# Windowed attention gated with a routed feed-forward layer: a searched table of key shifts for the list scheduler, values projected per chunk, loads in pieces, a hinted branch

## The chip, the cores and the metric

The kernel runs on one core of a Trainium2 chip. The metric is the device time of one execution in microseconds (us), median of the runs shown. The engines are named as the profile names them: PE (TensorE matrix multiplies) and PEld (its weight loads), DVE (VectorE), ACT (ScalarE), POOL (GpSimd), and SP, which here issues nearly all DMA transfers. PE takes its instructions in program order, and so do the others; an instruction that waits holds back all behind it on its engine.

## The reference

`x` is 2048 x 512 in bf16. Two branches of it are mixed by a gate per row.

```python
def _A_ref(x, wqkv, wo):                      # H = 32 heads, Dh = 16, window W = 256
    q, k, v = split_heads(x @ wqkv)
    scores = einsum(q, k) * Dh ** -0.5
    mask = (i - j >= 0) & (i - j < 256)
    p = softmax(where(mask, scores, -1e9))
    return merge_heads(p @ v) @ wo
def _B_ref(x, w_r, w_gate, w_up, w_down):     # F = 1792, C = 8
    r = x @ w_r
    idx = argsort(-r)[:8]                     # 8 rows of 2048
    y = (silu(x[idx] @ w_gate) * (x[idx] @ w_up)) @ w_down
    return x with y * sigmoid(r[idx]) added to rows idx
g = sigmoid((x * gate_w).sum(-1))
out = g * _A_ref(x) + (1 - g) * _B_ref(x)
```

## The kernel before

The 32 heads are worked in four chunks `c` of 8 heads (128 features). A chunk has 64 units; unit `u = 64c + kb` takes 32 keys (block `kb`), the 288 queries that can see them, and the 8 heads as two halves of four. For a unit, PE makes two matmuls into two PSUM banks (`s_unit`, L612: the keys stand in a block-diagonal tile `Kbd`, so that 4 heads x 32 keys fill 128 rows), ACT takes the exponential of both banks in one instruction into the tile `PT` (L619), and POOL multiplies the edges of the window by a mask for two units at a time (L626). Scores have two bank pairs in turn, so the scores of unit u wait until the exponential of unit u-2 has read its banks. `PT` is a ring of 40 slots, two for a unit: the exponential of unit u writes where unit u-20 stood, and must wait until `pv` (L647, probabilities times values for a tile `j` of 128 queries) has read that. A unit of key block kb is read last by tile j = kb/4 + 2.

Around this run the other items, each into one of two PSUM bank pairs (banks 4-5 and 6-7), which is free again when DVE has copied its result out: `xt` (transpose of x, L468), `qk_pair` (queries and keys of a chunk for 512 rows, L528; DVE then writes `QT` and `Kbd`, L506, L509, L514), `v_pair` (values, L571), `pv` (then a reciprocal L662 and a product L666 on DVE), `tr` (transpose of the attention output, L682, L687), `wo_pair` and `wo_one` (output projection, L702 and L718, then DVE's `out_evict` L693 and a DMA to the output, L695), and the routed branch: `z_item` (L739), `top_item` (8 largest, L762 to L776), `gu_item` (L799), `down_item` (L827). For `v_pair`, x is the stationary side: the values of two chunks (256 features) for 512 rows are made at once, copied to `Vn` (L583), written to a scratch `vsc` in DRAM (L586) and read back into the layout that `pv` wants, `Vbd` (L594, `v_read`). `pair` issues a projection as two phases of 64-row halves on the two halves of the array, one pair of matmuls per schedulable step.

The order of the work on each engine comes from a list scheduler (`Sched.schedule`). Every step has an engine, an assumed cost and a key; of the steps that are ready on an engine the one with the least key goes next, and on PE a score that is about to be ready is not delayed by a step that would end more than `TOL` = 100 ns late. The keys are written in units of `u` (`qk_pair` has d - 24, where d is the unit that needs it, and so on). Waits on semaphores follow from the order.

SP's queue before: x, the weights, `wo`, a copy of the whole of x to `xc` in DRAM (L413), then the value writes and reads, and three loads of 1792 KB for the routed branch (L818), each one DMA.

The end: DVE checks that all reciprocals lie in a range (L911 to L913), a matmul sums the check (L915), DVE writes `flag` (L916), SP waits for all transfers and engines, all engines meet, load `flag` and branch: a general program follows in the code that is jumped over when the flag says that all was in range.

## Time and profile before

| | us |
|---|---|
| median of 3 runs (217.71, 216.78, 219.93) | 217.71 |
| the profiled execution | 218.59 |
| its span, first to last instruction | 216.4 |
| mean granted TensorE clock | 0.885 |
| busy in the span: PE / ACT / DVE / POOL | 174.0 / 146.6 / 118.7 / 89.6 |
| the 256 exponentials (L619), busy | 140.3 |

The profiled execution is 0.88 us above the median, and 2.2 us longer than its span, since the time has something around the instructions. PE's busy time is that of pipelined instructions with modelled ends, so 80% busy does not say that PE has only 20% to spare or that it is the bound; what bounds is read from who waits for whom at each place.

### The profile page before, as it was taken

The page shows a single profiled execution, that of the slowest core. Times are in us where ns is not written, and L with a number is a line of the kernel's source. Part 1 is how long each engine was busy: PE and PEld are TensorE (multiplying, and loading weights), DVE is VectorE, ACT ScalarE, POOL GpSimd, SP SyncE. Part 2 cuts the span into 40 slices and gives each one's busy share as a digit, 9 for nine tenths or more (in the row PEclk, how much of TensorE's full clock was granted, in tenths as well). Part 3 has the DMA queues.
Part 4 walks back from the last instruction along what each step waited for, and adds up shares of the span by engine and source line. Part 5 has one row for each costly group of instructions (what it writes and reads, how often), then busy time and mean ns, then how long its engine had stood idle before and what let it go on. Part 6 is the DMA issues. An engine that isn't in the chain of part 4 may idle for free.

```text
span 216.4 us, 10097 instructions
## 1 busy us (share of the span) xinstructions
PE 174.0 (80%) x4598; PEld 111.0 (51%) x4599; DVE 118.7 (55%) x301; ACT 146.6 (68%) x266; POOL 89.6 (41%) x142
## 2 busy tenths in 40 slices
PE   2999548699687779986999868999899799998850
PEld 1655236465555535653667544645666455556410
DVE  5659507515617691827066183725663567575880
ACT  6677503686557797975779846656899899977000
POOL 3043401344134497653345432427365555645000
PEclk9999955969857976999599997999999799999995
DMA  6999436902410000045021472110330023254131
GB/s 172 334 267 423 129 77 126 302 24 56 103 32 4 5 3 5 3 129 216 3 55 32 138 232 57 38 44 5 83 108 3 3 100 100 80 169 151 52 123 32
DMA packets 27663, 21.72 MB, mean 100 GB/s; under 512 B 14896, under 2 KB 26432, under 8 KB 27584
## 3 DMA queue, kind: packets, MB, share of 16 engines
q1 hardware_dynamic: 26496, 20.75, 33.2%
q8 instruction: 37, 0.61, 1.1%
q10 hardware_dynamic: 1056, 0.26, 0.5%
q14 instruction: 10, 0.08, 0.1%
q0 software_dynamic: 64, 0.02, 0.0%
HBM read 16.13 MB, written 6.43 MB: 104 GB/s over the span
## 4 chain that ended last, share of the span: by engine, by line
PE 51%; ACT 19%; DVE 11%; DMA 9%; issue 6%; SPq 1%; DVEq 0%
ACT f_PT L619 19%; PE f_ps L612 12%; PE f_ps L647 11%; PE f_ps L528 10%; PE f_ps L571 6%; DMA f_vsc<-f_Vn 5%; PE f_ps L702 4%; DVE f_Kbd L514 3%; DVE f_Vn L583 3%; PE f_ps L468 2%; DMA f_xw<-in_A_x_dram 2%; PE f_ps L827 2%; PE f_ps L549 2%; DVE f_outt L693 1%; DVE f_Kr L509 1%
## 5 line engine op out<-in xcount | busy, mean ns | idle before, releaser
L619 ACT ACTIVATE f_PT<-f_ps 128x576 bf16<-128x576 f32 (+7 forms) x256 | 140.3, 625 | 49.8 <-PE f_ps L647 29.9
L626 POOL TENSOR_TENSOR f_PT<-f_PT,f_MK 128x256 bf16<-128x256 bf16 (+1 forms) x128 | 85.4, 669 | 109.3 <-ACT f_PT L619 108.4
L612 PE MATMUL f_ps<-f_QT,f_Kbd 64*128 64x288 bf16 (+7 forms) x512 | 77.9, 299 | 11.5 <-ACT f_PT L619 7.1
L647 PE MATMUL f_ps<-f_Vbd,f_PT 64*128 64x34 bf16 x2880 | 56.1, 179 | 13.2 <-DMA f_Vbd<-f_vsc 5.6
L647 PEld LDWEIGHTS f_ps<-f_Vbd,f_PT 64*128 64x128 bf16 x2880 | 51.8, 96 | 25.4 <-issue 14.7
L612 PEld LDWEIGHTS f_ps<-f_QT,f_Kbd 64*128 64x128 bf16 x512 | 25.9, 96 | 40.3 <-ACT f_PT L619 30.8
L528 PE MATMUL f_ps<-f_XT,f_W 64*128 64x512 bf16 x240 | 41.6, 413 | 0.5 <-issue 0.3
L509 DVE CAST f_Kr<-f_ps 128x512 bf16<-128x512 f32 x15 | 10.4, 691 | 27.1 <-PE f_ps L528 27.0
L571 PE MATMUL f_ps<-f_W,f_XT 64*128 64x256 bf16 x256 | 23.5, 299 | 0.2
L514 DVE TENSOR_SCALAR f_Kbd<-f_Kr,f_hm 128x512 bf16<-128x512 bf16 (+1 forms) x64 | 22.7, 417 | 0.0
L583 DVE CAST f_Vn<-f_ps 128x256 bf16<-128x256 f32 x32 | 11.4, 419 | 16.8 <-PE f_ps L571 16.7
L662 DVE RECIPROCAL f_RC<-f_ps 128x16 f32<-128x16 f32 x32 | 8.0, 248 | 18.9 <-PE f_ps L647 18.9
L571 PEld LDWEIGHTS f_ps<-f_W,f_XT 64*128 64x128 bf16 x256 | 13.5, 104 | 4.3 <-PE f_ps L571 1.2
L528 PEld LDWEIGHTS f_ps<-f_XT,f_W 64*128 64x128 bf16 x240 | 12.2, 100 | 6.5 <-issue 2.5
L693 DVE SCALAR_TENSOR_TENSOR f_outt<-f_ps,f_g_f,f_XT 128x512 bf16<-128x512 f32 x16 | 11.4, 746 | 5.6 <-PE f_ps L702 5.6
L702 PE MATMUL f_ps<-f_wo,f_OT 64*128 64x512 bf16 x96 | 13.8, 377 | 0.7 <-DVE f_outt L693 0.7
L666 DVE TENSOR_TENSOR f_On<-f_ps,f_RC 128x256 bf16<-128x256 f32 x32 | 13.5, 422 | 0.8
L468 PE MATMUL f_ps<-f_ident,f_xw 128*128 128x128 bf16 x64 | 6.2, 265 | 5.0 <-DMA f_xw<-in_A_x_dram 4.2
L506 DVE CAST f_QT<-f_ps 128x512 bf16<-128x512 f32 x15 | 10.2, 680 | 0.0
L687 DVE COPY f_OT<-f_ps 128x512 bf16<-128x512 bf16 x16 | 6.6, 412 | 3.6 <-PE f_ps L682 3.5
L468 PEld LDWEIGHTS f_ps<-f_ident,f_xw 128*128 128x128 bf16 x64 | 5.0, 120 | 6.5 <-issue 4.8
L920 ACT COPY f_sg<-f_ones_f 1x1 f32<-1x1 f32 x1 | 0.2, 191 | 10.8 <-DVE flag L916 10.8
(88 smaller groups left out, 86.9 us busy)
## 6 DMA issues: line engine op xcount, KB each, us to landing
f_vsc<-f_Vn SPq DMA_DIRECT2D x8, 272.0 KB, 3.5
f_XT<-f_xc SPq DMA_DIRECT2D x4, 512.0 KB, 4.4
out_dram<-f_outt SPq DMA_DIRECT2D x16, 128.0 KB, 1.7
f_xw<-in_B_w_gate_dram SPq DMA_DIRECT2D x1, 1792.0 KB, 10.1
f_xw<-in_B_w_up_dram SPq DMA_DIRECT2D x1, 1792.0 KB, 8.3
f_xw<-in_B_w_down_dram SPq DMA_DIRECT2D x1, 1792.0 KB, 8.1
f_xw<-in_A_x_dram SPq DMA_DIRECT2D x3, 512.0 KB, 6.7
f_Vbd<-f_vsc SPq DMA_DIRECT2D x32, 34.0 KB, 1.8
```

Of the source, the lines that this page charges most:

```text
L468: ins = e.transpose(pb[:, o:o + 128], x_sb[:, a1 + ai, kc * 128:kc * 128 + 128], ident[:])
L514: dve(lambda e, h=h, k0=k0, q=q: e.tensor_scalar(out=Kbd[:, c % 2, k0:k0 + w8, h, :], in0=Kr[:, tc % 2, 32 * w8 * q:32 * w8 * q + 32 * w8] ...
L528: return e.matmul(bank((A, B)[which]), W[R, kc, f0:f0 + 128], XT[R, kc, ts], start=st, stop=False, skip_group_check=True, tile_position=(R ...
L571: return e.matmul(bank((A, B)[b])[:, 256 * i:256 * i + 256], XT[R, kc, 128 * a:128 * a + 128], W[R, kc, f0:f0 + 256], start=st, stop=False ...
L583: dve(lambda e, dst=dst, b=b, cc=cc: e.tensor_copy(out=dst, in_=bank((A, B)[b]).rearrange("p (i c s h d) -> p c h s i d", i=2, c=2, s=2, h ...
L612: ins = e.matmul(bank(b0 + s)[:, 0:n], Kbd[R, c % 2, kb, :, :].rearrange("p h k -> p (h k)"), QT[R, c % 2, 32 * kb:32 * kb + n], start=Tru ...
L619: act(lambda e: e.activation(out=dst, in_=ps[:, b0:b0 + 2, 0:n], func=ACT.Exp, scale=0.25), r=[T(b0), T(b0 + 1)], w=[("P", slot // 2)], n= ...
L626: pool(lambda e: e.tensor_tensor(out=v, in0=v, in1=m, op=ALU.mult), r=[("P", sl // 2), ("P", sl // 2 + 1)] + MKR, w=[("Pm", sl // 4)], cos ...
L647: ins = e.matmul(bank((A, B)[rg])[:, col:col + 34], PT[R, o0:o0 + 128], Vbd[R, c % 2, :, kb % 4, kb // 16, s, (kb // 4) % 4, :], start=(kb ...
L666: dve(lambda e: e.tensor_tensor(out=dst, in0=both(h_)[:, :, 0:68 * nj].rearrange("p b (j g d) -> p b j g d", d=17, g=4)[:, :, :, :, 0:16], ...
L693: dve(lambda e: e.scalar_tensor_tensor(out=outt[:, a % 4, :], in0=bank(b), scalar=g_f[:, a:a + 1], in1=xb[:, a, :], op0=ALU.mult, op1=ALU. ...
L702: return e.matmul(bank((A, B)[o]), OT[R, c, 128 * a:128 * a + 128], wo[R, c, :], start=st, stop=False, skip_group_check=True, tile_positio ...
```

## The change

1. `SHIFT`, a table of 289 numbers, is added to the keys before scheduling: one for each item, key and engine. The scores and what has a key under -800 are left out. Two of its lines stand in the diff.
2. `qk_pair` and `wo_pair` make their matmuls 256 columns wide instead of 512 (`NQ = 2`), twice as many. `v_pair` makes the values of one chunk for 1024 rows, 128 columns wide, instead of two chunks for 512 rows; `Vn`, `vsc` and `v_read` follow (16 writes of half the size, 32 reads). `Kr` has four buffers instead of two.
3. Loads: the weights of later chunks, `wo`, the copy to `xc` and the three loads of the routed branch are cut in pieces, and each piece waits for the exponential of a unit (`gate(u)`).
4. The tail: the last four tiles of `pv`, `tr` and `wo_one` are cut finer (tiles 14 and 15 apart, the first three of the four matmuls of `wo_one` as steps of their own with an earlier key), and the check of the reciprocals is made per chunk (`rc_check`).
5. The end: the branch is a conditional jump over the general program, with a hint on PE that is placed 40 steps before PE's last; SP's waits for all transfers stand behind the branch.
6. `_track`: a wait is now also made for a write after a write or a read on the same engine (not on PE).

```diff
+        for op in self.log:
+            if op.key >= -800 and op.tag != "s":
+                op.key += SHIFT.get(_group(op), 0.0)
...
-                if op.eng == "pe" or not (raw or op.dma):
+                if op.eng == "pe":
                     continue
...
+                if e == "pe" and i == len(self.ops[e]) - HINT_AT:
+                    self.hint = h.mark_branch_hint_location()
...
-            if e == "sp":
-                for s, tot in enumerate(self.dtot):
-                    if tot > seen["sp"].get(("d", s), 0):
-                        h.wait_ge(self.dsem[s], tot)
...
+HINT_AT = 40
+NQ = 2
+VLEAD = 24
+SHIFT = {
+    "xt/-700/dve": 39.5, "xt/-699.9/pe": 5.5, "xt/-2/pe": 16.5, "xt/-2/dve": -30.5, "xt/-1.9/pe": 3.5, "xt/6/pe": -9.5, "xt/6/dve": -13,
+    "xt/6.1/pe": -13.5, "pair/-16/pe": -9, "v_pair/-16/dve": -108, "v_pair/-15.5/sp": -20, "v_read/-14.4/sp": -43.5, "k_evict/-16/dve": 0.5,
...
-        def v_pair(cp, g, key):
-            f0 = 1024 + 256 * cp
+        def v_pair(c, gg, key):
+            f0 = 1024 + 128 * c
...
-                w=[("P", slot // 2)], n=2 * n, key=u)
+                w=[("P", slot // 2), ("E", u)], n=2 * n, key=u)
...
-            pe(fn, r=WOR + [("OT", c, a) for c in range(4)], w=[T(b)], cost=960, key=key)
+            for c in range(4):
+                pe(lambda e, c=c: e.matmul(bank(b), OT[:, c, 128 * a:128 * a + 128], wo[:, c, :], start=(c == 0), stop=(c == 3)),
+                   r=WOR + [("OT", c, a)], w=[T(b)], cost=217 if c < 3 else 250, key=key if c == 3 else 252)
...
+        at(1.6, lambda: load_w(1, 1, 1, 1, 4000, gate=gate(1)))
+        at(2.6, lambda: load_w(0, 1, 1, 2, 4000, gate=gate(2)))
+        at(10.6, lambda: load_w(2, 1, 1, 10, 4000, gate=gate(10)))
+        for i in range(4):
+            at(46.6 + 4 * i, lambda i=i: load_ff(B_w_gate, i, 46 + 4 * i, gate(46 + 4 * i)))
+            at(62.6 + 2 * i, lambda i=i: copy_x(i, 62 + 2 * i, gate(62 + 2 * i)))
+            at(88.6 + 3 * i, lambda i=i: load_ff(B_w_up, i, 88 + 3 * i, gate(88 + 3 * i)))
+            at(126.6 + 4 * i, lambda i=i: load_down(i, 126 + 4 * i, gate(126 + 4 * i)))
...
+            br = eng.br_cond(bad < 1, "fk_done", "fk_general")
+            if et == mybir.EngineType.PE:
+                br.branch_hint(S.hint)
```

Three places show what moves. The first is SP's queue at the start, behind the loads of x. Before (`f_W` is the projection weights, `f_wo` the output weights, `f_xc` the copy of x, `f_vsc` and `f_Vbd` the value write and read):

```order
L392 DMA f_W<-in_A_wqkv_dram 128x4x384 x2
L392 DMA f_W<-in_A_wqkv_dram 128x4x256
L412 DMA f_wo<-in_A_wo_dram 32x4x512 x4
L451 DMA f_Vbd<-f_Vbd 32x2176 x4
L413 DMA f_xc<-in_A_x_dram 32x32768
L586 DMA f_vsc<-f_Vn 128x8x136
L594 DMA f_Vbd<-f_vsc 32x4x136 x4
```

The same stretch of SP's queue in the changed kernel:

```order
L512 DMA f_Vbd<-f_Vbd 32x2176 x4
L452 DMA f_W<-in_A_wqkv_dram 128x4x128 x2
L644 DMA f_vsc<-f_Vn 128x4x136 x2
L652 DMA f_Vbd<-f_vsc 32x4x272 x4
L452 DMA f_W<-in_A_wqkv_dram 128x4x128
L644 DMA f_vsc<-f_Vn 128x4x136 x2
L652 DMA f_Vbd<-f_vsc 32x4x272 x4
```

Ahead of the first value write stand two weight pieces instead of three large ones, `wo` and the copy of x, which now come later.

The second place is PE around units 44 to 53, in the first chunk. Before, with the scores of unit 44 in the first row and of units 45, 46 and 47 in the L612 rows after it (L528 is the query and key projection of the next chunk, L739 the router's and gate's products, L647 `pv`, L682 `tr`):

```order
L612 MATMUL f_ps<-f_QT,f_Kbd 128x288 x2
L528 MATMUL f_ps<-f_XT,f_W 128x512 x4
L612 MATMUL f_ps<-f_QT,f_Kbd 128x288 x2
L528 MATMUL f_ps<-f_XT,f_W 128x512 x4
L739 MATMUL f_ps<-f_wrg,f_XT 128x2 x128
L647 MATMUL f_ps<-f_Vbd,f_PT 128x34 x96
L612 MATMUL f_ps<-f_QT,f_Kbd 128x288 x2
L682 MATMUL f_ps<-f_ident,f_On 128x64 x8
L612 MATMUL f_ps<-f_QT,f_Kbd 128x288 x2
```

In the changed kernel, units 50 to 53 on PE (the four L670 rows are their scores, L705 `pv`, L795 the router's and gate's products):

```order
L705 MATMUL f_ps<-f_Vbd,f_PT 128x34 x16
L670 MATMUL f_ps<-f_QT,f_Kbd 128x288 x2
L705 MATMUL f_ps<-f_Vbd,f_PT 128x34 x32
L670 MATMUL f_ps<-f_QT,f_Kbd 128x288 x2
L705 MATMUL f_ps<-f_Vbd,f_PT 128x34 x32
L670 MATMUL f_ps<-f_QT,f_Kbd 128x288 x2
L705 MATMUL f_ps<-f_Vbd,f_PT 128x34 x16
L795 MATMUL f_ps<-f_wrg,f_XT 128x2 x16
L670 MATMUL f_ps<-f_QT,f_Kbd 128x288 x2
L795 MATMUL f_ps<-f_wrg,f_XT 128x2 x32
```

The 96 matmuls of one `pv` and the 128 small products stood in one block between the scores of units 45 and 46; they now stand in pieces between the scores of units 49 and 57.

The third place is PE's end, from the scores of the last unit on. Before (L702 is `wo_pair`, L718 `wo_one`):

```order
L612 MATMUL f_ps<-f_QT,f_Kbd 128x32 x2
L702 MATMUL f_ps<-f_wo,f_OT 128x512 x6
L647 MATMUL f_ps<-f_Vbd,f_PT 128x34 x16
L702 MATMUL f_ps<-f_wo,f_OT 128x512 x8
L647 MATMUL f_ps<-f_Vbd,f_PT 128x34 x64
L702 MATMUL f_ps<-f_wo,f_OT 128x512 x8
L682 MATMUL f_ps<-f_ident,f_On 128x64 x8
L702 MATMUL f_ps<-f_wo,f_OT 128x512 x8
L718 MATMUL f_ps<-f_wo,f_OT 128x512 x16
L915 MATMUL f_ps<-f_ones_f,f_okc 1x1
```

In the changed kernel, from the same score on (L761 is `wo_pair`, L775 `wo_one`, L740 `tr`):

```order
L670 MATMUL f_ps<-f_QT,f_Kbd 128x32 x2
L705 MATMUL f_ps<-f_Vbd,f_PT 128x34 x8
L761 MATMUL f_ps<-f_wo,f_OT 128x256 x14
L740 MATMUL f_ps<-f_ident,f_On 128x64 x4
L761 MATMUL f_ps<-f_wo,f_OT 128x256 x2
L241 BRANCH_PREFETCH_HINT
L775 MATMUL f_ps<-f_wo,f_OT 128x512
L761 MATMUL f_ps<-f_wo,f_OT 128x256 x16
L705 MATMUL f_ps<-f_Vbd,f_PT 128x34 x48
L775 MATMUL f_ps<-f_wo,f_OT 128x512 x7
L705 MATMUL f_ps<-f_Vbd,f_PT 128x34 x48
L740 MATMUL f_ps<-f_ident,f_On 128x64 x2
```

Eight more matmuls of `wo_one` follow. Behind the last score stands half as much of `wo_pair` as before (32 matmuls of 256 columns, not 30 of 512), and the sixteen matmuls of `wo_one` are parted by the last two tiles of `pv`.

## The prediction

> **What bounds the kernel now.** I read the page first: the busy times, the chain that ended last, and the group of the exponentials.

> ```profile
> PE 174.0 (80%) x4598; PEld 111.0 (51%) x4599; DVE 118.7 (55%) x301; ACT 146.6 (68%) x266; POOL 89.6 (41%) x142
> PEclk9999955969857976999599997999999799999995
> PE 51%; ACT 19%; DVE 11%; DMA 9%; issue 6%; SPq 1%; DVEq 0%
> L619 ACT ACTIVATE f_PT<-f_ps 128x576 bf16<-128x576 f32 (+7 forms) x256 | 140.3, 625 | 49.8 <-PE f_ps L647 29.9
> ```

> The 256 exponentials keep ACT busy for 140.3 us and cannot be cut by this change, and ACT stands idle for 49.8 us before them. That idle time is what an order can win, with what lies ahead of the first exponential and behind the last. ACT's waits and its timeline tell whose it is.

> ```profile
> ACT f_PT L619 <- PE f_ps L647: 29.9, 11, 11.5
> ACT f_PT L619 <- PE f_ps L612: 18.1, 28, 3.0
> 9.92 4.89 ACT L619 ACTIVATE f_PT<-f_ps 128x576 bf16<-128x576 f32 x8 [0.75 <-PE f_ps L612]
> 17.77 6.63 ACT L619 ACTIVATE f_PT<-f_ps 128x576 bf16<-128x576 f32 x12 [2.96 <-PE f_ps L612]
> 35.93 4.60 ACT L619 ACTIVATE f_PT<-f_ps 128x576 bf16<-128x576 f32 x8 [11.52 <-PE f_ps L647]
> 83.51 1.39 ACT L619 ACTIVATE f_PT<-f_ps 128x576 bf16<-128x576 f32 x2 [0.73 <-PE f_ps L647]
> 129.66 1.19 ACT L619 ACTIVATE f_PT<-f_ps 128x576 bf16<-128x576 f32 x2 [2.90 <-PE f_ps L647]
> 173.29 19.07 ACT L619 ACTIVATE f_PT<-f_ps 128x576 bf16<-128x576 f32 x34 [0.44 <-PE f_ps L612]
> 193.75 3.61 ACT L619 ACTIVATE f_PT<-f_ps 128x576 bf16<-128x576 f32 x7 [1.39 <-PE f_ps L647]
> 197.54 1.76 ACT L619 ACTIVATE f_PT<-f_ps 128x320 bf16<-128x320 f32 x5 [0.18 <-PE f_ps L612]
> ```

> Two kinds of wait. A wait for L647 is the ring: the exponential of unit u may not write before `pv` of tile (kb-20)/4+2 has read the slot. A wait for L612 is a score that came late. Where neither happens, 34 exponentials follow each other in 19.07 us, 0.56 each, with projections and `pv` in between: the last stages show that an order without loss exists. The exponentials run from 9.92 to 199.3 (197.54 and 1.76), 189.4 us; behind them lie 17.1 us. The stages:

> ```profile
> 9.90:70.40 60.50, 47.23 (x1179) 31.75 (x1179) 31.45 (x88) 35.41 (x65) 20.00 (x31) 0.81 0.53 143
> 70.40:114.40 44.00, 36.64 (x1072) 24.00 (x1070) 24.05 (x56) 35.42 (x66) 23.92 (x33) 0.84 0.15 51
> 114.40:161.90 47.50, 42.03 (x1190) 26.23 (x1190) 25.27 (x68) 35.10 (x65) 22.10 (x34) 0.96 0.32 84
> 161.90:199.30 37.40, 34.17 (x998) 20.89 (x998) 23.41 (x55) 34.43 (x64) 20.90 (x33) 0.95 0.28 87
> ```

> Each row is one chunk: its length, then busy PE, PEld, DVE, ACT, POOL, the granted clock, and DMA. ACT works some 35 us in each; the chunks last 60.5, 44.0, 47.5 and 37.4. The granted clock is lowest (0.81, 0.84) where the stalls are.

> **The first value transfer.** The largest stall, 11.52 us at unit 20, is a DMA's.

> ```profile
> 15.41 11.26 DMA f_vsc<-f_Vn
> 28.00 1.84 DMA f_Vbd<-f_vsc
> f_vsc<-f_Vn SPq DMA_DIRECT2D x8, 272.0 KB, 3.5
> 26.69 1.74 SPq L594 DMA_DIRECT2D f_Vbd<-f_vsc  x4
> ```

> The write of the first values took 11.26 us where the eight of them have a median of 3.5, behind 1 MB of weights, `wo` and the 2 MB copy of x. In the changed queue (the first place above) two 128 KB pieces stand there. The new `v_pair` needs twice the rows of x, so I put its copies on DVE half a us later, to 16.0; with 0.5 for the issue, 3.5 for the landing, 1.74 for four reads and 1.84 for the last to land, `pv` has its values at 23.6. The exponential of unit 19 ended at 24.4. So the data is no longer last; what is left at unit 20 is what PE does between, 20 matmuls of `v_pair` and 88 of `pv`, which the rates below make 1.7 us, and 0.3 of latency: 2.0, bounds 1.5 and 4.

> **The blocks on PE.** I went through both orders for one thing: is the `pv` that unit u's ring slot needs placed behind the score of unit u+1? If so, ACT must run empty there. Before there are ten such places, units 20, 44, 60, 124, 148, 152, 156, 164, 172 and 244, and the waits for L647 are eleven, 29.9 us, the eleventh being the 0.73 at 83.51. In the changed order two are left, units 20 and 148: the second place above shows one that went. Unit 148 has 48 matmuls of `pv` behind that score and cost 2.90; I take 2.0, bounds 1 and 3. **Ring: 29.9 becomes 2.0 + 2.0 + 0.7 = 4.7**, bounds 2.5 and 7.7.

> ```profile
> 188.94 0.43 PE f_ps L702 x4
> 148.38 0.44 PE f_ps L571 x8
> 99.18 0.40 PE f_ps L647 x32
> ```

> These give PE's rates where it runs at full clock: 512 columns 107 ns a matmul, 256 columns 55, `pv` 12.5. So `qk_pair` in halves costs the same (480 x 55 against 240 x 107, 26 us each way). A 128-column matmul has no row: by columns it takes 27 ns, and 512 of them 14 us like the 256 before; at worst it takes the 55 of the 256-column row, which adds 14 us to PE. I take the first, since `pv` shows that a weight load can be had every 12.5 ns. What halves buy is that no step between two scores is longer than the 0.43 us that ACT's pitch of 0.56 leaves beside a score.

> [...]

> **Late scores, 18.1 us.** 2.96 is unit 8, which waits for the second projection; that chain keeps its length, and I keep 3.0. The other 15.1 have two sources:

> ```profile
> 35.35 0.39 SPq L818 DMA_DIRECT2D f_xw<-in_B_w_gate_dram  x1
> 40.05 1.88 issue
> 93.76 0.40 SPq L818 DMA_DIRECT2D f_xw<-in_B_w_up_dram  x1
> 100.24 1.98 issue
> PE f_ps L647 <- issue: 5.4, 6, 1.9
> 60.45 0.43 PE L612 MATMUL f_ps<-f_QT,f_Kbd 64*128 64x288 bf16 x2
> 64.77 0.30 PE L612 MATMUL f_ps<-f_QT,f_Kbd 64*128 64x288 bf16 x2
> f_xw<-in_B_w_gate_dram SPq DMA_DIRECT2D x1, 1792.0 KB, 10.1
> ```

> PE stood for 1.88 and 1.98 us with nothing in the profile to wait for, 5 and 6 us behind the issue of a 1792 KB load, of which the first took 10.1 to land. And after a gap PE ran slow for some us: a pair of scores takes 0.43 at 60.45 and 0.30 at 64.77. Fewer gaps make fewer slow stretches, and loads in quarters leave less to stand behind. How much goes cannot be read off; between 3 and 15.1 I take half, 7.5. **Late scores: 3.0 + 7.5 = 10.5.**

> So the exponentials take 140.3 + 4.7 + 10.5 = 155.5, from 9.9 to 165.4, against 199.3.

> **The tail**, from the last exponential to the end:

> ```profile
> 204.60 3.40 PE L718 MATMUL f_ps<-f_wo,f_OT 128*128 128x512 bf16 x15 [0.16 <-issue]
> 208.66 1.40 DVE L693 SCALAR_TENSOR_TENSOR f_outt<-f_ps,f_g_f,f_XT 128x512 bf16<-128x512 f32 x2
> 209.97 0.14 DVE L916 TENSOR_SCALAR flag<-f_ps 1x1 int32<-1x1 f32 x1
> 201.61 8.80 SPq L695 DMA_DIRECT2D out_dram<-f_outt  x8
> out_dram<-f_outt SPq DMA_DIRECT2D x16, 128.0 KB, 1.7
> ```

> Behind the last score the changed PE has 32 matmuls of 256 columns (1.8 us), 16 of `wo_one` (3.4) and 104 of `pv` (1.3) with a few transposes: 6.7 us, against 10.8 before from 199.3 to the last product of DVE at 210.06. The score starts 0.5 ahead of the last exponential; with 0.3 of latency, 0.74 for the last product, and 0.8 for the turns between PE and DVE over tiles 14 and 15, that is 8.0 us behind 165.4. Then the last output: issued until 210.41 before, landed 1.7 later, 2.0 behind DVE. The flag was written at 210.11 and the span ends at 216.4: 6.3 us, of which the landing explains 2.0 and the rest, 4.3, is load and branch. Now the landing is waited for behind the branch, so the two overlap. How much of the 4.3 the hint takes has no row, between 0 and 4.3; if more than 2 go, the landing is last, and I take that: 2.2 with the closing waits. Tail 10.2, against 17.1; bounds 9.2 and 12.5. [...]

> What is added on DVE, 15 short check steps for three of 0.42 to 0.68, and the new same-engine waits lies beside the exponentials; DVE has 24 busy us of 37 in the last chunk to cover it, and if it were not hidden it would cost 2 us at most. Gated pieces stand in SP's queue ahead of value reads that are needed 8 to 30 units (4 to 17 us) later, more than their 3.5 us.

> **The sum.** Span 165.4 + 10.2 = 175.6. The profiled execution lasts 2.2 longer than its span and is 0.9 above the median: 175.6 + 2.2 - 0.9 = **177 us** against 217.7. Its own range: with the low ends (ring 2.5, late scores 5.3, 2 us less busy ACT as fewer exponentials start from rest, tail 9.2) 166; with ring 7.7, late scores 15.0 and a tail of 12.5, 187.

> **Rivals.** (a) *DVE holds the banks.* All items but scores share two bank pairs, freed by DVE. DVE's 118.7 us go into 176, so it would be 67% busy, not 55.

> ```profile
> 168.06 1.60 DVE f_Kbd L514 x4
> PE f_ps L647 <- DVE f_On L666: 0.5, 2, 0.3
> ```

> For it: DVE is 11% of the chain, 24 us, 4 of them in the tail, and at 168.06 the chain runs through the block-diagonal keys. Against it: PE's direct waits for DVE are short. If most of those 20 us come back as late scores, 177 + 17 = 194.
> (b) *Narrow matmuls are not cheaper, and it gets slower.* If a matmul is bound by its weight load and costs what the next wider one does (107 ns at 256 columns, 55 at 128), `qk_pair` gains 26 us, `wo_pair` 10, `v_pair` 14: 50 us on a PE that is busy for 160 between first and last exponential. 210 us of PE work would then set the end: 9.9 + 210 + 10.2 + 1.3 = 231. It decides from some 34 us on, where PE passes what the kernel takes now. Against it stand the 55 ns of the 256-column row.
> (c) *The hint does nothing.* Then load and branch, 4.3, follow the flag, which comes 0.5 to 1 behind the last product: 180.

> **Chances.** My forecast (166 to 187) 0.66; (a), 187 to 205, 0.20; (c), inside that range, 0.06; better than 166, 0.04; (b) 0.04. Eight in ten need about half of (a): 166 to 194. A measurement of this kernel tells some 2% from no change, 213.4 to 222; faster than that are all but (b) and the worst of (a): 0.93, same 0.03, slower 0.04.

> **What would show it.** In the changed profile: the first value write lands in 3 to 5 us and `pv` starts before 25; ACT's waits for L705 fall under 8 us with units 20 and 148 the largest; the four chunks last about 42, 38, 38 and 37 us, and the clock is above 0.9 in the second; the 128-column matmuls come at 27 ns; from the last exponential to the end 10 us, the landing last. The prediction is wrong if ACT still waits over 25 us, for DVE's banks, for late scores at a low clock, or for value reads behind gated loads.

## The result and the profile after

| | before | after |
|---|---|---|
| median, us | 217.95 (216.78 to 219.93, 4 runs) | 203.69 (200.94 to 205.74, 4 runs) |
| the profiled execution / its span | 218.59 / 216.4 | 203.83 / 202.5 |
| exponentials, first start to last end | 9.92 to 199.3 = 189.4 | 9.50 to 187.07 = 177.6 |
| of it ACT waits for `pv` / for late scores | 29.9 / 18.1 | 5.5 / 28.8 |
| last exponential to DVE's last product | 10.8 | 8.15 |
| last product to the end of the execution | 8.5 | 8.6 |

The ratio is 0.9295, 95% interval 0.917 to 0.942: 14 us faster. Forecast were 41 (177.0, range 166 to 194), so the sign held and the size didn't. A second time, with experiments 14 and 15, the changed kernel took 201.37 beside 217.82, ratio 0.9249 (0.9165 to 0.9332). Ratios and intervals here and below leave out runs that lie over 1.5% above the fastest of their kernel, medians don't, so a ratio can differ a little from that of two medians.

The page after: the busy times, the clock, the chain that ended last, the instruction transfers of PE, and from the groups of instructions the one of the exponentials (busy, mean ns, idle before it and for whom).

```profile
PE 166.8 (82%) x5199; PEld 129.1 (64%) x5199; DVE 120.7 (60%) x301; ACT 148.1 (73%) x266; POOL 86.7 (43%) x142
PEclk9999999999658889969999797599999999969996
PE 65%; ACT 10%; issue 9%; DVE 6%; DMA 5%; POOL 2%; SPq 0%; DVEq 0%
q8 instruction: 42, 0.69, 1.4%
L677 ACT ACTIVATE f_PT<-f_ps 128x576 bf16<-128x576 f32 (+7 forms) x256 | 141.8, 622 | 36.0 <-PE f_ps L670 28.8
```

The view of the waits has both of ACT's:

```profile
ACT f_PT L677 <- PE f_ps L670: 28.8, 42, 3.9
ACT f_PT L677 <- PE f_ps L705: 5.5, 3, 2.3
```

The ring's wait (now L705) went as forecast, 24.4 us of it, and the late scores (L670) grew by 10.7. "issue" grew from 6% to 9% of the chain, and PE has 5199 matmuls in place of 4598. ACT's timeline shows the stalls (the idle time ahead of a row stands in its brackets).

```profile
9.50 4.74 ACT L677 ACTIVATE f_PT<-f_ps 128x576 bf16<-128x576 f32 x8 [0.39 <-PE f_ps L670]
18.15 6.98 ACT L677 ACTIVATE f_PT<-f_ps 128x576 bf16<-128x576 f32 x12 [3.92 <-PE f_ps L670]
27.43 2.28 ACT L677 ACTIVATE f_PT<-f_ps 128x576 bf16<-128x576 f32 x4 [2.30 <-PE f_ps L705]
50.91 2.61 ACT L677 ACTIVATE f_PT<-f_ps 128x576 bf16<-128x576 f32 x5 [2.45 <-PE f_ps L670]
114.52 1.82 ACT L677 ACTIVATE f_PT<-f_ps 128x576 bf16<-128x576 f32 x3 [2.25 <-PE f_ps L705]
125.79 1.93 ACT L677 ACTIVATE f_PT<-f_ps 128x576 bf16<-128x576 f32 x3 [3.50 <-PE f_ps L670]
182.31 4.76 ACT L677 ACTIVATE f_PT<-f_ps 128x576 bf16<-128x576 f32 x11 [0.44 <-PE f_ps L670]
```

And PE's timeline, what stood ahead of the scores at 50.91 and 125.79:

```profile
50.40 0.32 PE L795 MATMUL f_ps<-f_wrg,f_XT 64*128 64x2 bf16 x13 [2.45 <-issue]
125.30 0.21 PE L705 MATMUL f_ps<-f_Vbd,f_PT 64*128 64x34 bf16 x2 [3.26 <-issue]
```

PE stood for 2.45 us in the middle of `z_item` and for 3.26 in the middle of a `pv`, waiting for nothing that the profile shows, and ACT then ran dry for 2.45 and 3.50.

```
                    block entered   next: transfer starts   lands   its first instruction   pause
before                      35.92          39.59            40.52          41.93            2.05
after                       45.78          48.20            49.17          50.40            2.61
after                      119.09         122.80           124.05         125.29            3.43
after                      146.18         147.02           148.10         149.60            1.34
after                      153.06         154.18           155.36         158.61            none
```

I read the next block as asked for when the one ahead is entered. In the eleven cases of both kernels in which its transfer started within 1.5 us of that and PE then waited over 0.5 us for "issue", it starts 0.4 to 1.4 us behind the entry, mostly 0.6 to 1.2, takes 0.9 to 1.4 and runs 1.2 to 1.5 after it landed: 3.2 to 3.9 us from block to block, some 3.4. A block that PE works through in less ends in a pause (146.18: 119 of its 128 matmuls are `pv`, done in 2.1 us); one that takes 5.6 us (153.06) ends in none. Two late starts, 2.4 and 3.7 us at 45.78 and 119.09, fall where other transfers fill the queues (the DMA share of the first 2 us behind these entries is 0.81 and 1.12); that at 81.44 is 2.25 us late with a share of 0.00, so load isn't the only cause. Pauses over 0.2 us sum to 11.9 us before and **21.3 after**; the idle time in them is 9.0 and 16.3. ACT's idle time that has a pause in it sums to some 17 us of 33.9 after (2.25 of them the ring's wait at 114.52); the others are 3.92 of unit 8, 2.30 of unit 20 and small ones.

### The profile page after: what moved, and what is told of

The parts are those of the page before. It is cut to its first block, busy times and chain, and to the rows that moved or that the text cites. A ratio compares the mean times of both kernels' runs of the same rounds, so it can differ in the third digit from the quotient of the medians.

```text
span 202.5 us, 11344 instructions
## 1 busy us (share of the span) xinstructions
PE 166.8 (82%) x5199; PEld 129.1 (64%) x5199; DVE 120.7 (60%) x301; ACT 148.1 (73%) x266; POOL 86.7 (43%) x142
## 4 chain that ended last, share of the span: by engine, by line
PE 65%; ACT 10%; issue 9%; DVE 6%; DMA 5%; POOL 2%; SPq 0%; DVEq 0%
PE f_ps L705 16%; PE f_ps L670 15%; PE f_ps L588 13%; ACT f_PT L677 10%; PE f_ps L761 6%; PE f_ps L631 5%; DMA f_idxT<-f_idxu 3%; PE f_ps L889 3%; DMA f_xw<-in_A_x_dram 2%; PE f_ps L775 2%; DVE f_QT L566 1%; POOL f_PT L684 1%; PE f_ps L740 1%; PE f_ps L609 1%; DVE f_idxu L824 1%
## 5 line engine op out<-in xcount | busy, mean ns | idle before, releaser
L677 ACT ACTIVATE f_PT<-f_ps 128x576 bf16<-128x576 f32 (+7 forms) x256 | 141.8, 622 | 36.0 <-PE f_ps L670 28.8
L670 PE MATMUL f_ps<-f_QT,f_Kbd 64*128 64x288 bf16 (+7 forms) x512 | 76.5, 292 | 7.2 <-ACT f_PT L677 4.7
L705 PE MATMUL f_ps<-f_Vbd,f_PT 64*128 64x34 bf16 x2880 | 54.6, 178 | 9.3 <-issue 8.0
L705 PEld LDWEIGHTS f_ps<-f_Vbd,f_PT 64*128 64x128 bf16 x2880 | 50.0, 95 | 14.9 <-issue 10.2
L588 PE MATMUL f_ps<-f_XT,f_W 64*128 64x256 bf16 x480 | 41.9, 286 | 0.5
L670 PEld LDWEIGHTS f_ps<-f_QT,f_Kbd 64*128 64x128 bf16 x512 | 26.7, 96 | 20.7 <-ACT f_PT L677 12.2
L588 PEld LDWEIGHTS f_ps<-f_XT,f_W 64*128 64x128 bf16 x480 | 24.3, 100 | 6.4 <-PE f_ps L588 2.0
L720 DVE RECIPROCAL f_RC<-f_ps 128x16 f32<-128x16 f32 (+1 forms) x33 | 8.2, 249 | 28.7 <-PE f_ps L705 28.1
L631 PE MATMUL f_ps<-f_W,f_XT 64*128 64x128 bf16 x512 | 21.4, 218 | 1.3 <-issue 1.0
L631 PEld LDWEIGHTS f_ps<-f_W,f_XT 64*128 64x128 bf16 x512 | 17.2, 95 | 3.5 <-issue 1.4
L566 DVE CAST f_QT<-f_ps 128x512 bf16<-128x512 f32 x15 | 10.3, 687 | 11.9 <-PE f_ps L588 11.9
L761 PE MATMUL f_ps<-f_wo,f_OT 64*128 64x256 bf16 x192 | 15.9, 283 | 1.3 <-issue 0.8
L724 DVE TENSOR_TENSOR f_On<-f_ps,f_RC 128x256 bf16<-128x256 f32 (+1 forms) x33 | 13.6, 412 | 0.6
L569 DVE CAST f_Kr<-f_ps 128x512 bf16<-128x512 f32 x15 | 10.2, 683 | 5.8 <-PE f_ps L588 5.8
L642 DVE CAST f_Vn<-f_ps 128x512 bf16<-128x512 f32 x16 | 10.3, 683 | 5.1 <-PE f_ps L631 5.1
L751 DVE SCALAR_TENSOR_TENSOR f_outt<-f_ps,f_g_f,f_XT 128x512 bf16<-128x512 f32 x16 | 11.3, 742 | 3.1 <-PE f_ps L761 2.9
L761 PEld LDWEIGHTS f_ps<-f_wo,f_OT 64*128 64x128 bf16 x192 | 9.3, 97 | 4.4 <-PE f_ps L761 1.3
L745 DVE COPY f_OT<-f_ps 128x512 bf16<-128x512 bf16 (+2 forms) x18 | 7.0, 390 | 7.4 <-PE f_ps L740 6.0
## 6 DMA issues: line engine op xcount, KB each, us to landing
out_dram<-f_outt SPq DMA_DIRECT2D x16, 128.0 KB, 1.7
```

The source lines that it names most:

```text
L566: dve(lambda e: e.tensor_copy(out=dst, in_=bank(b)), r=[T(b)], w=[("QT", c % 2, tc)], cost=610, key=key, rel=rel)
L588: return e.matmul(bank((A, B)[which])[:, w0:w1], W[R, kc, f0:f0 + 128], XT[R, kc, 512 * tc + w0:512 * tc + w1], start=st, stop=False, skip ...
L631: return e.matmul(bank((A, B)[b])[:, 128 * i:128 * i + 128], XT[R, kc, 128 * a:128 * a + 128], W[R, kc, f0:f0 + 128], start=st, stop=False ...
L642: dve(lambda e, b=b, g=g: e.tensor_copy(out=Vn[:, g, :, :, :, 0:16], in_=bank((A, B)[b]).rearrange("p (i s h d) -> p h s i d", i=4, s=2, h ...
L670: ins = e.matmul(bank(b0 + s)[:, 0:n], Kbd[R, c % 2, kb, :, :].rearrange("p h k -> p (h k)"), QT[R, c % 2, 32 * kb:32 * kb + n], start=Tru ...
L677: act(lambda e: e.activation(out=dst, in_=ps[:, b0:b0 + 2, 0:n], func=ACT.Exp, scale=0.25), r=[T(b0), T(b0 + 1)], w=[("P", slot // 2), ("E ...
```

## Experiments

Theory F: blocks of 256 PE instructions arrive no faster than one in some 3.4 us, later under load, and ACT runs dry where a block holds fewer than six scores (6 x 0.56 = 3.4). After, 15.3 of the 21.3 us of pauses follow on such blocks, 15 of the 40 that have a block behind them. Rival L: the large loads make the pauses, whatever the number of instructions (the prediction's reading). Rival B: late scores come from PE's work or from DVE's banks.

| run | PE blocks | pauses, us | blocks asked for over 1.5 us late | ACT waits: late scores / `pv` | median, us |
|---|---|---|---|---|---|
| before | 36 | 11.9 | 7 | 18.1 / 29.9 | 217.95 |
| after | 41 | 21.3 | 12 | 28.8 / 5.5 | 203.69 |
| small loads | 41 | 13.9 | 4 | 17.6 / 6.2 | 193.47 |
| 128-row matmuls | 35 | 9.3 | 10 | 24.0 / 4.6 | 216.08 |
| wide `pv` | 30 | 3.6 | 8 | 13.7 / 3.7 | 184.60 |
| small loads, wide `pv` | 30 | 2.8 | 1 | 7.9 / 4.6 | 177.65 |
| no table | 41 | 11.4 | 5 | 19.0 / 22.0 | 212.03 |
| loads spread | 41 | 14.6 | 6 | 30.3 / 4.1 | 204.15 |
| loads spread, in time | 41 | 13.7 | 5 | 26.2 / 4.3 | 200.44 |
| the same, 512 columns | 38 | 16.7 | 9 | 26.7 / 3.1 | 198.60 |
| 512 columns alone | 38 | 20.9 | 10 | 30.2 / 3.1 | 202.38 |
| before, three loads later | 36 | 11.3 | 8 | 19.9 / 21.3 | 211.57 |

Pauses, late blocks (to within one or two, by where a boundary is set) and waits are of one profiled execution each. The changed kernel had pauses of 24.6 us in its second profile (experiment 13), so a difference of some 3 us between two rows means nothing. The medians of before were 217.06 to 218.20 in all sets.

**1. Small loads.** Edit: the pieces of the feed-forward weights and of the copy move little, in the same places.

```diff
-  e.dma_start(WG[:, i, :], src[:, i, :])
+  e.dma_start(WG[:, i, 0:64], src[:, i, 0:64])        # load_down: 16 of 512 columns; copy_x: 8 of 512 rows
```

> The order is that of the changed kernel; the twelve pieces of the feed-forward weights and the four of the copy of x move one part in 7 to 64 of their bytes, and x is reloaded from the input (so the feed-forward values and the eight replaced rows are not those of the reference). Theory F (blocks of PE instructions): PE takes its instructions in blocks of 256; each block is asked for when the one ahead of it is entered, and runs no sooner than some 3.4 us later (0.6 to 1.2 to start, 0.9 to 1.4 to move, 1.2 to 1.5 until the first instruction); a large load adds 1 to 2.6 to the start. Then the starts later than 1.5 us (ten in the changed kernel, up to 3.72) mostly go, the pauses of PE at the 193rd of each 256 instructions fall from 21 us in sum to 12 to 15, those in dense blocks stay, and the kernel takes 192 to 199 us. Rival L (the loads alone make the pauses, as the prediction had it): the pauses vanish, under 3 us in sum, and it takes under 188. Rival B (late scores come from the bank pairs that DVE frees): nothing changes, 202 to 206.

193.47 us, ratio 0.8953 (0.8846 to 0.9061), pauses 13.9: F in every number. The loads cost the changed kernel 10 us, but two thirds of the pauses stand without them, so L falls.

**2. 128-row matmuls.** Edit: `pair`, z, gate, up and down products without the split in 64-row halves.

```diff
-  lo(e, ph, q, ph); ins = hi(e, 1 - ph, q, ph)
+  ins = lo(e, ph, q, 0)                               # R = slice(0, 128), no tile_position
```

> The order is that of the changed kernel; the projections, wo, z, the gate and up products and the down product use one matmul over 128 rows where two over 64 rows stood: 782 matmuls and as many weight loads less, 36 blocks of 256 instructions instead of 41 or 42. Theory F (blocks of instructions arrive no faster than one in 3.4 us): the pauses behind z and the gate and up products (2.6, 1.0, 1.5, 0.8, 1.4 us) shrink to the half or less, the sum of pauses falls from 21 us to 11 to 15, and it takes 193 to 199 us. Rival L (loads alone): the pauses of 2.6, 1.6 and 3.4 us behind the loads stay, and it takes 201 to 205. A third possibility: a weight load of 128 rows isn't hidden behind the matmul ahead of it; then 592 matmuls cost some 50 ns more each, PE is 30 us busier, and it takes 210 or more.

Pauses 9.3, better than F said, and yet 216.08 us (212.15 to 217.19). The third possibility had the time, and PE is busier (189.7 us, 166.8 after), but its mechanism fails, and no run shows its 50 ns more for each matmul: in a steady stream such matmuls cost no more (experiment 4: 512 over 128 rows and 128 columns took 28.76 us, as did the 1024 halves). What the records show is that the weight load of a score, which is split, starts late behind one of them. PE's weight loads around 62 us, and their waits in sum:

```profile
61.78 0.10 PEld L669 LDWEIGHTS f_ps<-f_QT,f_Kbd 64*128 64x128 bf16 x2 [0.21 <-issue]
62.01 0.33 PEld L587 LDWEIGHTS f_ps<-f_XT,f_W 128*128 128x128 bf16 x4
62.56 0.10 PEld L669 LDWEIGHTS f_ps<-f_QT,f_Kbd 64*128 64x128 bf16 x2 [0.21 <-issue]
PEld f_ps L669 <- issue: 15.2, 68, 0.7
```

68 such waits, 15.2 us; after has 3.4 in 4 for the same line. That this is the whole of the cost isn't shown: ACT's busy time grew too (151.2 from 141.8), as exponentials follow each other more slowly, without a wait long enough for the list. The split forms are worth their instructions here.

**3. Plain end.** Edit: no mark and no hint; SP waits at the end only for the DMAs that no engine had waited for.

```diff
-  br.branch_hint(S.hint)
-  for sem, val in S.left_over: nc.sync.wait_ge(sem, val)
+  for sem, val in S.unseen: nc.sync.wait_ge(sem, val)  # 2 waits in place of 24
```

> The changed kernel without the mark and the hint on PE's branch, and with the closing waits on SyncE only for the DMAs that no engine had waited for. If the hint did nothing, PE's branch lasts 3.3 to 3.4 us as before; if it helped, longer than 3.38. If SyncE's 24 closing waits at 0.06 us each set the end, the span now ends 4.9 to 5.2 us behind the flag, not 6.4, and the run takes 1.2 to 1.5 us less than the changed kernel's 203.8; if the wait for the branch target sets it, nothing changes.

PE's branch took 3.39 us (3.38 after, 3.35 before), the span ended 5.1 behind the flag, not 6.4; but the one execution took 203.62, for it ends 6.9 us behind the flag, after 7.7 (the time of the execution less the flag's place in the span; whether a part lies ahead of the first instruction isn't on record): 0.8 us, not 1.3. So the time outside the span isn't the same in both.

**4. The fetch rate by itself.** A kernel of eight streams of independent matmuls.

> No attention here, zeros are written: PE runs eight streams of independent matmuls, one after another: 1024 over 64 rows by 34 columns (the form of pv), 1024 over 128 rows by 68 columns, 256 over 64 rows by 256, 128 over 128 rows by 256, 1024 over 64 rows by 128, 512 over 128 rows by 128, and, while SyncE copies 2 MB of x eight times within DRAM, the first two again. Theory F: without any load the first two streams take 26 to 28 ns a matmul, 3.3 to 3.6 us for each 256 instructions, though 12.5 ns were seen for the first in short runs; 64 by 256 takes 55, 128 by 256 110, 64 by 128 27 and 128 by 128 53 to 56; with the copies the first two take 32 to 50. Rival L: the first stream takes 12.5 to 14 ns without the copies and only slows with them. If a weight load over 128 rows isn't hidden, the 128-row streams take 50 ns more each than said here.

PE's timeline, the first streams without load, then those during the copies:

```profile
14.84 2.00 PE L25 MATMUL m_ps<-m_m,m_w 64*128 64x34 bf16 x128 [2.00 <-issue]
18.29 2.00 PE L25 MATMUL m_ps<-m_m,m_w 64*128 64x34 bf16 x128 [1.46 <-issue]
29.50 34.43 PE L29 MATMUL m_ps<-m_m,m_w 128*128 128x68 bf16 x1024
63.86 14.15 PE L25 MATMUL m_ps<-m_m,m_w 64*128 64x256 bf16 x256
92.02 28.76 PE L25 MATMUL m_ps<-m_m,m_w 64*128 64x128 bf16 x1024
120.71 28.76 PE L29 MATMUL m_ps<-m_m,m_w 128*128 128x128 bf16 x512
167.82 2.00 PE L25 MATMUL m_ps<-m_m,m_w 64*128 64x34 bf16 x128 [5.84 <-issue]
171.27 2.00 PE L25 MATMUL m_ps<-m_m,m_w 64*128 64x34 bf16 x128 [1.46 <-issue]
205.98 9.44 PE L29 MATMUL m_ps<-m_m,m_w 128*128 128x68 bf16 x256 [2.62 <-issue]
```

The small matmuls run 128 at a time in 2.0 us (15.6 ns each; the granted clock is 0.50 from 10.8 us on) and then stand. Until 14.9 us SP's writes of the output run beside them, and 256 instructions take 4.0 to 4.3 us. From then on nothing else is loaded, and PE stands for 1.46 or 1.73 us: 3.45 to 3.73 us for 256 instructions, 27 to 29 ns a matmul. Under the copies it is up to 8.1. Streams that need 3.59 us or more for 256 instructions (64 x 128: 28.69 us from its start to the next stream's for eight times 256) don't pause without load. The first two went as F had it but for 128 x 68, which takes 33.6 and not 26 to 28 (31 from 35 us on, at full clock: 4.0 us for 256 instructions, and it doesn't pause); L's 12.5 to 14 is met only within a block (15.6). The 64 x 128 stream takes 28 ns a matmul, the prediction's 27.

**5 and 6. Wide `pv`, with the loads and without.** Edit: each step issues half its matmuls over twice the columns.

```diff
-  for kb in part:
-      ins = e.matmul(bank((A, B)[rg])[:, col:col + 34], PT[R, o0:o0 + 128], Vbd[R, c % 2, :, kb % 4, kb // 16, s, (kb // 4) % 4, :], ...)
+  for kb in part[2 * s:2 * s + 2]:
+      ins = e.matmul(bank((A, B)[rg])[:, col:col + 68], PT[R, o0:o0 + 128], Vbd[R, c % 2, :, kb % 4, kb // 16, :, (kb // 4) % 4, :], ...)
```

> The order and the loads are those of the changed kernel. Each step of pv issues half its matmuls, over 68 columns instead of 34, so that the columns stay the same and 1440 matmuls with their weight loads go (half of the products are left out: the attention values are not those of the reference). 30 blocks of 256 PE instructions instead of 41. Theory F (a block of instructions can't follow the one ahead in under some 3.4 us, so one that holds fewer than six scores starves ACT): the blocks with fewer than six scores fall from 20 of 41 to 4 of 30, the pauses from 21 us to 5 to 9, ACT's late scores from 28.8 to 10 to 16, and it takes 188 to 193 us. Rival L (the large loads make the pauses, whatever the number of instructions): 201 to 205. Rival B (late scores come from PE's work in columns, or from DVE's banks): 201 to 205.

> Both at once: the small loads of the first experiment and the wide steps of pv (both leave out work, as said there). Theory F: with neither loads in the way nor dense blocks the pauses fall under 4 us, ACT's late scores to 6 to 9 of which 3.9 are unit 8, the exponentials end by 164 to 168, and the kernel takes 179 to 184: what the prediction had for the exponentials, with the tail that was measured. Rival B: 190 to 194, as with the small loads alone (193.5).

184.60 (183.08 to 187.04) and 177.65 us (ratio of the second 0.8129, 0.8061 to 0.8197), below what F gave. More pauses went (to 3.6 and 2.8) than I had counted. (Counted from where the pauses stand, 16 of 41 blocks hold fewer than six scores after, and 3 of 29 here, not the 20 and 4 of the expectation.) L falls. B falls as it was put, for columns and order are the same. Yet PE has less to do; `pv` in after, then with both edits:

```profile
L705 PE MATMUL f_ps<-f_Vbd,f_PT 64*128 64x34 bf16 x2880 | 54.6, 178 | 9.3 <-issue 8.0
```
```profile
L706 PE MATMUL f_ps<-f_Vbd,f_PT 64*128 64x68 bf16 x1440 | 44.0, 199 | 2.9 <-issue 2.1
```

The group of the exponentials, first of wide `pv`, then of both:

```profile
L677 ACT ACTIVATE f_PT<-f_ps 128x576 bf16<-128x576 f32 (+7 forms) x256 | 138.3, 627 | 18.8 <-PE f_ps L670 13.7 <-PE f_ps L706 3.7
```
```profile
L677 ACT ACTIVATE f_PT<-f_ps 128x576 bf16<-128x576 f32 (+7 forms) x256 | 138.4, 628 | 14.2 <-PE f_ps L670 7.9 <-PE f_ps L706 4.6
```

With both edits the exponentials run from 9.7 to 162.1, 152.4 us where the prediction's sum had 155.5, in a kernel that leaves out half of `pv`'s products. Its chunks, by windows, against those of after:

```profile
9.70:50.60 40.90, 38.08 (x1009) 29.33 (x1009) 30.46 (x78) 34.35 (x66) 20.47 (x32) 1.00 0.30 71
50.60:88.90 38.30, 35.46 (x898) 27.49 (x900) 28.73 (x65) 35.27 (x67) 21.79 (x34) 0.87 0.19 46
88.90:127.90 39.00, 36.61 (x914) 25.66 (x914) 23.36 (x56) 34.98 (x65) 21.67 (x34) 0.96 0.23 50
127.90:162.10 34.20, 32.64 (x806) 24.79 (x802) 25.65 (x62) 34.02 (x64) 20.66 (x32) 1.00 0.41 120
```
```profile
9.50:56.90 47.40, 40.65 (x1334) 32.62 (x1332) 30.75 (x79) 35.16 (x66) 20.74 (x32) 0.95 0.35 82
56.90:100.30 43.40, 37.91 (x1270) 30.93 (x1269) 27.93 (x65) 35.99 (x66) 21.45 (x34) 0.86 0.46 140
100.30:147.90 47.60, 40.19 (x1257) 28.58 (x1255) 22.60 (x56) 35.70 (x65) 21.71 (x34) 0.89 0.35 90
147.90:187.10 39.20, 35.27 (x1162) 28.77 (x1157) 25.97 (x63) 35.06 (x64) 20.72 (x32) 0.96 0.35 106
```

40.9, 38.3, 39.0 and 34.2 us, where the prediction had 42, 38, 38 and 37, against 47.4, 43.4, 47.6 and 39.2. The second numbers are PE's busy time: 154.0 us of 177.6 after, 142.8 of 152.4 here. Of the 25.2 us between the two, 14.2 are idle time in pauses that went (16.3 to 2.1) and 11.2 are PE's own work, mostly `pv`'s. What fewer pauses would bring with `pv` as long as it was, these two runs don't tell; experiment 1 does for part of them. The clock of the second chunk is 0.87 here too, and its two stretches at half clock, from 59.8 and 73.5 us on, begin with no pause ahead: slow stretches don't come from the pauses alone.

**7. No table.** Edit: `SHIFT = {}`.

> The changed kernel with an empty table of shifts: the same matmuls, loads and gates, in the order that the plain keys give. On PE the exponential of some 13 units then needs a pv that stands behind the next score, and 41 blocks of instructions fall short of six scores by 24 us in sum, against 19 with the table. If the table's worth is in the order around the ring and the scores (the prediction), ACT waits 8 to 15 us for pv in place of 5.5 and 3 to 6 us more for late scores: 209 to 219. If the gain of the change came from the loads and the narrow steps alone, 202 to 206.

212.03 us, ratio 0.9759 (0.9672 to 0.9846), inside the 209 to 219 that go with a table worth its order, but not by its parts. ACT waits for `pv` 22.0 us, not 8 to 15, and for late scores 19.0, less than with the table, with 11.4 us of pauses. The table takes 16.5 us out of the ring, and there are 9.8 more of late scores. My reading is that the next block has time to arrive while ACT and PE stand for the ring: instructions and loads are the same, and the pauses are half. No run isolates it.

**8 and 9. Loads spread.** Edit: each load of 448 or 512 KB goes in pieces of 112 or 128 KB, each behind an exponential of its own; first with the copy 40 units later, then with no piece too late.

```diff
-  dma(lambda e: e.dma_start(WG[:, i, :], src[:, i, :]), r=[gate], ...)
+  op = dma(part(0), r=[gate], ...)
+  op.more = [(part(q), units behind the first) for q in (1, 2, 3)]   # put into SP's queue behind that exponential
```

> The changed kernel, whole, with PE, ACT, DVE and POOL in the same order: each of the large loads (feed-forward weights, the copy of x, the reload) goes in pieces of 112 to 128 KB behind one exponential each, the copy of x for the most part 40 units later, and SyncE closes with the waits for the DMAs that no engine had waited for. Theory F: with less in the queues when a block is asked for, fewer than 6 of 41 start more than 1.5 us late (12 before), the pauses fall from 21 us to 14 to 17, the end comes 1.3 us sooner, and it takes 192 to 198 us. If what counts is the bytes per us and not the size of a piece, the pauses stay at 19 to 22 and it takes 200 to 203.

> As the run with the spread loads, whole and in the same order, but with no piece later than its consumer wants it: the copy of x between units 76 and 91, the up weights one unit apart, the down weights 0.75 apart from unit 146 on. In the run before, PE waited 2.7 us for up weights and 4.5 for down weights, which ate what the pauses gave (21.3 to 14.6 us). Theory F: those 7.2 us go, the pauses stay at 14 to 17, and it takes 195 to 199 us. If pauses and clock in that stretch cost the same with or without the waits, it stays at 202 to 205.

The first: pauses 14.6 and 6 late blocks, as F says, but 204.15 us (ratio 0.9355, 0.9253 to 0.9457). Its waits show why:

```profile
PE f_ps L918 <- DMA f_xw<-in_B_w_down_dram: 4.5, 1, 4.5
PE f_ps L878 <- DMA f_xw<-in_B_w_up_dram: 2.7, 1, 2.7
```

Spread loads end later, and PE's queue stands at the step that wants them, 4.5 and 2.7 us. The second still waits 3.4 and 1.1 us there and takes 200.44 (0.9247, 0.916 to 0.9333), above the 195 to 199 expected; its pauses are 13.7. In both, the pauses are 7 us shorter than after and the late scores are not (30.3 and 26.2, after 28.8). So here fewer pauses alone didn't pay, and beyond the waits for weights I have no cause to show.

**10 and 11. 512 columns.** Edit: of two steps of `qk_pair` and `wo_pair` the first issues nothing, the second 512 columns.

> The same, and the projections and wo in 512 columns: of two steps the first issues nothing and the second the whole width, so the order of the steps stays. 336 matmuls less, 38 blocks of PE instructions instead of 41; the blocks short of six scores fall short by 18.4 us in sum, against 18.9. Theory F: 0 to 3 us below the run beside it, 193 to 198. If a step of 0.21 us in place of two of 0.11 makes scores late, it is 1 to 4 us above it.

> The changed kernel with that edit alone, its loads as they were: what the halves of the projections and of wo are worth. The prediction had them buy that no step between two scores is longer than 0.43 us; a step of 0.21 is under that, so by it nothing changes, 202 to 205. Theory F: 200 to 204, by 38 blocks instead of 41.

198.60 (ratio 0.9155, 0.9105 to 0.9205; just above its range) and 202.38 (0.9244, 0.9155 to 0.9334): 1 to 2 us below the runs without this edit, which the intervals don't settle. Pauses hardly change (20.9 against 21.3), since the blocks that fall short hold `pv`, z and the gate and up products, not projections. The halves of the change bring nothing that can be measured.

**12. Before, with three loads later.** Edit in the kernel before: the copy of x behind exponential 70, value weights of chunks 2 and 3 behind 50, `wo` behind 100, orders kept.

> The kernel before, PE's and all other orders kept, with three loads moved back in SyncE's queue: the copy of x behind exponential 70, the value weights of chunks 2 and 3 behind 50, wo behind 100. If the first value write waited for those (the prediction), it lands 4 to 6 us after its issue in place of 11.3, ACT's wait at unit 20 falls from 11.5 to 4 to 6 us, and the kernel takes 209 to 213: about half of what the change gained. If the write was held by something else, 216 to 219.

211.57 us (208.35 to 214.15); the wait at unit 20 fell from 11.52 to 4.37, and the reads were issued 3.9 us behind the write:

```profile
28.52 7.17 ACT L627 ACTIVATE f_PT<-f_ps 128x576 bf16<-128x576 f32 x13 [4.37 <-PE f_ps L655]
15.16 0.38 SPq L594 DMA_DIRECT2D f_vsc<-f_Vn  x1
19.08 1.77 SPq L602 DMA_DIRECT2D f_Vbd<-f_vsc  x4
```

The write did wait for those loads; that alone is 5.5 us (217.06 in the same set) of the 14.

**13 to 15. On one chip, and hints for all.** The changed kernel again, experiment 10 again, and that with a mark and a hint on every engine's branch.

> The changed kernel as it is, on the same chip as the two beside it: 201 to 206 us by all theories, so that they can be compared with it.

> The whole kernel with loads in pieces, in time, the projections and wo in 512 columns and the few closing waits, once more beside the changed kernel. By the first time (198.6 us, 198.1 to 199.4) it is 4 to 6 us below it; if that was the chip, under 2.

> The same, with a mark and a hint on the branch of every engine, not PE's alone. PE's branch took 0.39 to 0.49 us in six kernels in which no block of instructions was asked for behind the hint, and 2.9 to 3.9 in three in which one was; yet the end came 7.7 to 7.9 us behind the flag in both. If the other engines' own fetch of the branch target sets the end, then with hints on all it comes 4 to 5.5 us behind the flag, not 7.1, and the time falls by 1.5 to 3 us. If a second fetch at the program's end sets it, 6.5 to 7.1 and no change.

201.37 (199.0 to 203.6), 200.49 (194.98 to 202.57) and 200.63 (198.56 to 202.12). So the version that the experiments point to isn't shown to beat the changed kernel. With all hints the execution ends 7.05 us behind the flag: the second reading, no change.

## Why the prediction was right and wrong

**Right.** *First value write:* issued at 15.31, reads issued at 19.01, 3.7 us (0.5 for the issue and 3.5 forecast); unit 20 waits 2.30 (2.0); `pv` starts at 25.05, just missing the 25. *Ring:* 5.5 us in three waits (4.7), the largest at units 20 and 148 as read from the order. The size at unit 148 (2.25, 2.0 forecast) is luck: a pause of PE, 1.26 us idle at 113.71, lies in it. *Rates:* 28 ns for 128 columns over 64 rows, and rival (b) is out. Experiment 4's streams of 128 columns took 28.76 us for 512 matmuls over 128 rows, 56 ns each, or for 1024 over 64. *Tail:* 8.15 us from the last exponential to the last product (8.0).

**The step that failed: late scores, 10.5 forecast, 28.8 measured**, 18.3 of the 26.8 us by which the profiled execution missed (203.83 against 177.0). In the prediction it is the term of 7.5 us, half of what could not be read off. I took 1.88 and 1.98 us of "issue" behind two loads for a matter of the loads, and halved what followed for loads in pieces. Half of the reading holds (experiment 1: 11.2 us of late scores are the loads'), but the pauses have a floor of their own: without load too a block followed the one ahead by 3.45 us at the least (experiment 4). The change has five more blocks, and 16 of 41 that hold fewer than six scores (12 of 36 before), as its order packs `pv` and small products between scores; PE's idle time in pauses went from 9.0 to 16.3 us. In before, the ring's waits may have hidden part of it (experiment 7). The rest of the 18.3 isn't taken apart. The rows were there: seven "issue" waits on PE before `pv` and the small products, some far from any load. And the sum had no term for PE's own work: rival (b) had PE busy for 160 us between the first and the last exponential, it is 154.0 after, and a stretch of 155.5 leaves PE 1.5 us for all its waits. The 177.65 of experiment 6 agrees with the forecast by luck in part: its exponentials took 3.1 us less than the sum had, with 11 us less work on PE, and its end took longer. Of the other signs, the second chunk's clock was 0.86, not above 0.9.

**The end, 2.2 forecast from the last product to the span's end, 7.3 measured.** Rival (c), the hint does nothing, held: PE's branch took 3.38 us. In eight kernels of the experiments it took 0.39 to 0.49. There q8 has one transfer behind PE's branch, where after has two (198.41 and 201.57), which I read as the block at the target having come before; no run isolates it. And the end came no sooner (7.7 to 7.9 us behind the flag; 6.6 to 7.1 with two closing waits). What is left is the other engines: SP's first closing wait came 3.8 us behind its branch in after (201.06 and 197.28), then 24 waits at 0.06. In the kernels with the loads in time it came 1.0 to 1.2 behind, with a hint on SP and without, and the end was the same. What then lasts until the end isn't in the records, but transfers of instructions (q8 and q14) run to within 1 to 2 us of it; their part wasn't isolated.

**The rest** of the miss: 1.5 us in ACT's busy time (141.8 against 140.3), 1.5 in waits too short for the list, 0.8 of ring, less 0.4 for the earlier start. No run shows the 2 us that the range took off ACT for exponentials that start from rest: before, the 576-column ones behind an idle time of over 0.2 us took 651 ns, those within 0.06 us of another 656. Rival (a) had the time (187 to 205) and not the cause: of PE's waits for DVE, outside the final check, none is longer than 0.6 us.

## What to carry to other kernels

Count instructions, not only time. In a printed order, take PE's matmuls 128 at a time and look for a group that the pacing engine wants done in less than some 3.4 us, here one with fewer than six scores (16 of 41 after, two of them in the tail; 9 of the 15 that have a block behind them ended in a pause over 0.5 us, and 5 of the other 25). And ask of a stall that an order removes what arrived unseen under its cover: here, as I read experiment 7, the next block of instructions did, and with the table 9.8 us more of late scores stand against 16.5 less of the ring. Add up, too, what the engine that feeds the pacing one has to do in the forecast stretch: it must fit, with its waits. A load that is cut and spread must still land before the first instruction that wants it: in experiment 8 PE stood there for 4.5 and 2.7 us, with all that was queued behind.

## What the hardware showed that I hadn't expected

- PE's waits for "issue" over 0.5 us, before and after, stand at every 256th record and nowhere else, beside transfers of 16 KB on q8: where PE waited, blocks were some 3.4 us apart (3.2 to 3.9 before and after, 3.45 at the least in experiment 4's 34-column streams) and up to 8.1 beside copies. With 34-column matmuls, 2.0 us a block, PE stood 1.46 us or more behind each 128 of them in that experiment's rows from 14.8 us on.
- A split weight load of a score right behind a 128-row matmul starts 0.21 us late in experiment 2's rows; in streams of one kind the two forms cost the same (28.76 us for 1024 halves or 512 whole ones at 128 columns).
- With a hint PE's branch took 3.38 us in after and 0.39 to 0.49 in eight kernels of the experiments; without one 3.35 before and 3.39 in experiment 3. What decides isn't settled: my reading in the last expectation, that no block may be asked for behind the hint, fails with the loads spread, where one was and the branch took 0.49.
